# A buffer of its own for the last head's rows of wo, and kept keys in wo's fourth place

## The chip, the cores and the metric

The kernel runs on one core of a Trainium2 chip. The metric is the device time of one execution in microseconds, lower is better. Before the change three runs gave a median of 1353.76 us (1351.77 to 1354.28).

## The reference

One token goes through two equal rounds of attention over a cache of 8192 keys and values and an MLP, with the same weights in both rounds. All arrays are float32.

```python
B, Sq, D = 1, 1, 640
H, Sk, Dh = 32, 8192, 128            # Dff = 1728

def _A_ref(x, k_cache, v_cache, wq, wo):
    q = (x @ wq).reshape(B, Sq, H, Dh).transpose(0, 2, 1, 3)
    scores = jnp.einsum("bhqd,bhkd->bhqk", q, k_cache) * (Dh ** -0.5)
    p = _softmax(scores, axis=-1)
    o = jnp.einsum("bhqk,bhkd->bhqd", p, v_cache)
    return o.transpose(0, 2, 1, 3).reshape(B, Sq, H * Dh) @ wo

x = x + _A_ref(_layernorm(x), k_cache, v_cache, wq, wo)
x = x + relu(_layernorm(x) @ w1) @ w2
# and both lines once more
```

A head's keys and values are 8.39 MB, all heads' 268 MB, and each round needs all of them; what still lies on the chip from the first round needn't be read again in the second. A head's rows of wo are a block of 128 x 640, 327,680 bytes.

## The kernel before

**Loops.** `attention_and_mlp(L, ...)` is called for L = 0 and L = 1, called layers here. Layer 0 takes the heads from 0 to 31, layer 1 from 31 to 0. For each head the scores (line 433: `ps`, from keys and the spread query), a softmax, and the product with the values (line 484: `outs`) follow each other on TensorE, with VectorE and ScalarE in between.

**The ring.** Keys and values come in units (`UNITS`, line 41 on): a unit is one transfer and consists of pieces, each with its own products. A piece ("k", (r, c, n)) is n of 512 columns of quarter r. Most heads have two units of 4096 KB; heads 28 to 31 are cut finer. The units lie in one large buffer, `ring`, of RING = 4248 places (one place is 8 float32 in each of 128 partitions). `pump` (line 141) issues transfers on SP's queue in a fixed order as long as `place` (line 126) finds room; `release`, called when a piece's last product is recorded, frees its places and calls `pump`. In layer 0 the stream uses places 0 to 3072; the rest is for what stays.

**What stays.** `KEPT` and all units of heads 30 and 31 are read once, in layer 0, and used again in layer 1: `(29, 0)` are 176 columns of keys of head 29 (88 places), `(29, 5)` a quarter of a block of values (64 places). They lie from EDGE = 4096 on. In layer 1 `pieces_of` (line 195) takes a head's kept units first. The four units of head 29's keys that are not kept go, for layer 1, into buffers that the MLP of layer 0 no longer needs (`load_beside`, line 175: `mix`, `wct` and two parts of `w2_t`).

**wo.** The rows of wo come in groups of four heads, HG = 4, into one buffer `wo_t` (`load_wo`, line 211; 1280 KB, on ACT's queue but for the first). When a group's four heads are done, `run_out` (line 626) multiplies their outputs into `acc` (line 402) and then issues the load of the next group into the same buffer. That happens in the scores of the next group's first head: group 7 is loaded in head 28 of layer 0, and stays for the first four heads of layer 1. The layer's last head is multiplied on its own in `mlp` (line 766). Its rows are also needed early, for a product of wo and w1 (`mixing`, line 539); for that they are loaded a second time into `mix[:, :D]` (line 676), where VectorE then changes them in place.

**Side work.** `due` queues such jobs; `side_work` puts the next part of a job between two pieces of a head.

**Order and counters.** Each engine takes its instructions in the order of the program; so do the two queues, SP's and ACT's. Each transfer counts up one of eight counters (DMAHW0 to DMAHW7 in the listings) when it has landed. They are given out in turn over the transfers of both queues, in program order, so a transfer is not issued before the one eight places ahead has landed, whichever queue that was on.

Of the kernel before, what the change touches and what calls it, by code (L numbers as in the profile page):

```python
# [10 lines left out]
F32 = mybir.dt.float32  # L11
AF = mybir.ActivationFunctionType
ALU = mybir.AluOpType
AX = mybir.AxisListType

P = 128
D = 640
H = 32
# [5 lines left out]
HG = 4  # L24
NG = H // HG
# [8 lines left out]
RUN = COLS // 4  # L34
# [6 lines left out]
UNITS = {h: WHOLE for h in range(H)}  # L41
UNITS[0] = HALVES[:2] + LAST
UNITS[1] = HALVES
UNITS[29] = [
    ("k", [(0, 0, 176)]),
    ("k", [(0, 176, 336), (1, 0, 96)]),
    ("k", [(1, 96, 160)]),
    ("k", [(1, 256, 256), (2, 0, 384)]),
    ("k", [(2, 384, 128), (3, 0, RUN)]),
    ("v", [(0, 0, 1)]),  # L50
    ("v", [(0, 1, 3)]),
    ("v", V_ALL[1:2]),
# [2 lines left out]
UNITS[30] = HALVES  # L55
UNITS[28] = [("k", K_ALL[:1]), ("k", K_ALL[1:2])] + HALVES[1:]
UNITS[31] = HALVES[:2] + LAST
KEPT = [(29, 0), (29, 5)]
BESIDE = 4
RING = 4248  # L60
WC_AT = [5, 8]
MIX_AT = [[7, 9, 11, 13], [12, 16, 20, 24]]
FLAT = 3072
# [3 lines left out]
def wide(kind, piece):  # L67

    return 4 * piece[2] * (1 if kind == "k" else DH) // 8


def size(unit):
    return sum(wide(unit[0], piece) for piece in unit[1])
# [14 lines left out]
def decode_kernel(ctx: ExitStack, tc: tile.TileContext, x, kv, wq, wo, w1, w2, out):  # L88
    nc = tc.nc
    consts = ctx.enter_context(tc.tile_pool(name="consts", bufs=1))  # L90
# [10 lines left out]

    ring = consts.tile([P, 8 * RING], F32, name="ring")
    order = [(h, i) for h in range(H) for i in range(len(UNITS[h]))]
    kept = [u for u in order if u[0] > KEPT[0][0] or u in KEPT]
    assert sum(size(UNITS[h][i]) for h, i in kept) <= RING
    todo = [(0, u) for u in order]
    todo += [(1, (h, i)) for h in range(H)[::-1] for i in range(len(UNITS[h])) if (h, i) not in kept]

    beside = todo[len(order) : len(order) + BESIDE]
    del todo[len(order) : len(order) + BESIDE]  # L110
    dram_at, o = {}, 0
    for h, i in order:
        dram_at[h, i] = o
# [2 lines left out]
    at_of = {}  # L116
# [9 lines left out]
    def place(layer, u, n):  # L126


        step = 8 if u in KEPT else max(m for m in (8, 64, 256, 512) if n % m == 0)
        low, high = 0, RING if layer else FLAT  # L130
        if layer == 0 and u in kept and (u in KEPT or u[0] == 30 and UNITS[30][u[1]][0] == "k"):
            low, high = (EDGE, RING) if u in KEPT else (FLAT, EDGE)
        at, best = low, None
# [37 lines left out]
    def more_of_w2(a, b, where):  # L171
        rows = W2_LAST if a == FB - 1 else P
        nc.sync.dma_start(where[:rows], w2[:rows, a:b])

    def load_beside(i, where, n):
        (layer, u), at = beside[i], 0
        kind, pieces = UNITS[u[0]][u[1]]
        assert 8 * size(UNITS[u[0]][u[1]]) == n
        nc.sync.dma_start(
            where[:, at : at + n],  # L180
            kv[dram_at[u] : dram_at[u] + P * n].rearrange("(p m) -> p m", p=P),
        )
        for t, piece in enumerate(pieces):
            at_of[layer, u, t] = where, at
            at += 8 * wide(kind, piece)
# [18 lines left out]
    wq_t, wo_t = {}, {}  # L204
# [3 lines left out]
        wq_t[g] = t.rearrange("p (c n) -> p c n", c=NB)  # L208
        queue.dma_start(t, wq[P * g : P * g + P])

    def load_wo(g, queue):
        wo_t[g] = wts.tile([P, HG, D], F32, name="wo_t")
        queue.dma_start(wo_t[g], wo[g])

    xr = work.tile([P, DR], F32, name="xr", bufs=2)
    load_wq(0, nc.sync)
    nc.scalar.dma_start(xr, x)
    pump()
    load_wo(0, nc.sync)

    ones = consts.tile([P, 1], F32, name="ones")
    nc.vector.memset(ones, 1.0)
# [17 lines left out]
    w1_t = consts.tile([P, NB, DFF], F32, name="w1_t")  # L240
    w2_t = consts.tile([P, SLOTS, D], F32, name="w2_t")
    mix = consts.tile([P, DFF], F32, name="mix")
    wct = consts.tile([P, NB, P], F32, name="wct")


# [45 lines left out]
    def centred(xt, s):  # L291

        pt = columns(xt)
        mean(pt, s)
        yield "dve"
        return less_mean(pt, pt[:, :NB])
# [102 lines left out]
    def times_rows(acc, wt, col, first, last):  # L399

        for g in range(4):
            nc.tensor.matmul(  # L402
                acc[32 * g : 32 * g + 32, :DR],
                col.to_broadcast([col.shape[0], 32]),
                wt[:, g * DR : (g + 1) * DR],
                start=first,
                stop=last,
                skip_group_check=True,
            )
# [116 lines left out]

    o_cols = {}

    def projected(acc, run, cols, first, last):
        for j, h in enumerate(run):  # L530
            times_rows(
                acc,
                wo_t[h // HG][:, h % HG],
                cols[:, j : j + 1],
                first and j == 0,
                last and j == len(run) - 1,
            )

    def mixing():

        wc = mix[:, :D]
        s = work.tile([P, 1], F32, name="m_s")
        nc.vector.tensor_reduce(s, wc, AX.X, ALU.add)
        nc.vector.scalar_tensor_tensor(
            wc, s.to_broadcast([P, D]), -1.0 / D, wc, op0=ALU.mult, op1=ALU.add
        )
        yield "pe"
        pt = ps_m.tile([P, 512], F32, name="px")
        for c in range(4):
            nc.tensor.transpose(pt[:, c * P : (c + 1) * P], wc[:, c * DR : c * DR + P], ident)  # L550
        yield "dve"
        nc.scalar.copy(wct[:, :4].rearrange("p c d -> p (c d)"), pt)
        yield "pe"
        pt = ps_m.tile([P, 512], F32, name="px")
        for g in range(4):
            nc.tensor.matmul(
                pt[32 * g : 32 * g + 32, :P],
                wc[:, g * DR + P : (g + 1) * DR],
                ident,
                start=True,  # L560
                stop=True,
            )
        yield "dve"
        nc.scalar.copy(wct[:, 4], pt[:, :P])
# [28 lines left out]
    def attention_and_mlp(L, xr, s, before=None):  # L593

        heads = list(range(H))[:: 1 - 2 * L]
        last = heads[-1]
        runs = [heads[a : a + HG] for a in range(0, H, HG)]
        groups = [run[0] // HG for run in runs]
        runs[-1] = runs[-1][:-1]

        acc = ps_m.tile([P, 512], F32, name="acc")
# [18 lines left out]
        def queries_of(k):  # L620
            yield from wide_queries(groups[k], xc, r)
            yield "dve"
            if k + 1 < NG:
                load_wq(groups[k + 1], nc.scalar)

        def run_out(k):

            projected(acc, runs[k], o_cols[k], k == 0, False)
            yield "dve"
            load_wo(groups[k + 1], nc.scalar)  # L630

        def first_of_last():
            projected(acc, runs[-1][:2], o_cols[NG - 1], False, False)
            yield "dve"

        mlp_in = []

        def before_last():

            projected(acc, runs[-1][2:], o_cols[NG - 1][:, 2:], False, True)  # L640
            yield "dve"
            xp = work.tile([P, DR], F32, name="xr", bufs=2)
            sp = work.tile([P, 1], F32, name="x_s", bufs=2)
            nc.vector.scalar_tensor_tensor(
                xp, acc[:, :DR], 1.0, xr, op0=ALU.mult, op1=ALU.add, accum_out=sp
            )
            yield "pe"
            xpc = yield from centred(xp, sp)
            yield "pe"
            ph = ps_m.tile([P, 512], F32, name="acc")  # L650
            mlp_in.extend([xp, ph])
            for c in range(NB):
                hidden(ph, xpc[:, c : c + 1], w1_t[:, c], c == 0, False)
                if c < NB - 1:
                    yield "pe"

        def due(h):

            where = heads.index(h)
            k, j = divmod(where, HG)  # L660
            if j == 0:
                o_cols[k] = work.tile([P, HG], F32, name="o_cols", bufs=2)
            if where and j == 0:
                chores.append([run_out(k - 1), "pe"])
            if j == 2 and k + 1 < NG:
                slow.append([queries_of(k + 1), "pe"])
            if where == H - 2:
                chores.append([first_of_last(), "pe"])
            if where == H - 1:
                chores.append([before_last(), "pe"])  # L670
            if L == 0 and where == H - HG:
                slow.append([centre_query(NG - 1, HG - 1), "pe"])
            if L == 0 and where == 4:
                nc.scalar.dma_start(w1_t, w1)
            if where == WC_AT[L]:
                nc.scalar.dma_start(mix[:, :D], wo[last // HG][:, last % HG])
            if where == WC_AT[L] + 1:
                slow.append([mixing(), "dve"])
            if where in MIX_AT[L]:
                slow.append([mixing_quarter(MIX_AT[L].index(where)), "pe"])  # L680
# [28 lines left out]
        for where, h in enumerate(heads):  # L709
# [21 lines left out]
            if h == last:  # L731
                o = work.tile([P, 1], F32, name="c_ol")
# [16 lines left out]
            else:  # L749
                k, j = divmod(where, HG)  # L750
# [8 lines left out]
    def mlp(L, o, last, xp, ph):  # L759
# [3 lines left out]
        if L == 0:  # L763
            more_of_w2(SLOTS, 10, mix[:, : 2 * D].rearrange("p (b d) -> p b d", d=D))
        pd = ps_m.tile([P, 512], F32, name="pm")
        times_rows(pd, wo_t[last // HG][:, last % HG], o, True, True)
        in_wait(64)

        hr = wct.rearrange("p c d -> p (c d)")[:, : 2 * P]
# [99 lines left out]
        cols = work.tile([P, NB], F32, name="x_cols")  # L869
        nc.vector.tensor_copy(cols, pt[:, :NB])  # L870
        pq = ps_m.tile([P, 512], F32, name="px")
        for c in range(NB):
            g = c % 4
# [22 lines left out]
    s = work.tile([P, 1], F32, name="x_s", bufs=2)  # L896
# [84 lines left out]
```

## Time and profile before

| | |
|---|---|
| median of three runs | 1353.76 us |
| profiled execution | 1351.81 us, of it 1349.9 us span |
| TensorE busy | 909.9 us, 67% of the span |
| VectorE busy | 297.2 us, 22% |
| ScalarE busy | 58.5 us, 4% |
| moved by the transfers | 573.71 MB, mean 425 GB/s |
| mean granted clock of TensorE | 0.799 |

The page cuts the span into 40 equal slices of 33.7 us; its row "DMA" gives the busy share of the 16 DMA engines in tenths, its row "GB/s" what they moved. The chain of waits follows the work that ended last back to what released it; a share of "DMA" in it is time in which the next step waited for a transfer to land. q1 is SP's queue and q10 ACT's; their rows give packets, MB, and the share of the 16 engines' span.

### The profile page before, as it was taken

The page shows a single profiled execution, that of the slowest core. Times are in us where ns is not written, and L with a number is a line of the kernel's source. Part 1 is how long each engine was busy: PE and PEld are TensorE (multiplying, and loading weights), DVE is VectorE, ACT ScalarE, POOL GpSimd, SP SyncE. Part 2 cuts the span into 40 slices and gives each one's busy share as a digit, 9 for nine tenths or more (in the row PEclk, how much of TensorE's full clock was granted, in tenths as well). Part 3 has the DMA queues.
Part 4 walks back from the last instruction along what each step waited for, and adds up shares of the span by engine and source line. Part 5 has one row for each costly group of instructions (what it writes and reads, how often), then busy time and mean ns, then how long its engine had stood idle before and what let it go on. Part 6 is the DMA issues. An engine that isn't in the chain of part 4 may idle for free.

```text
span 1349.9 us, 14049 instructions
## 1 busy us (share of the span) xinstructions
PE 909.9 (67%) x6078; PEld 282.3 (21%) x6078; DVE 297.2 (22%) x979; ACT 58.5 (4%) x147; POOL 2.9 (0%) x10
## 2 busy tenths in 40 slices
PE   5564676766667666666688776677566767668667
PEld 2111121211112112112143211222112221122113
DVE  2121121222112222122223222221121212212212
ACT  0000000000000000000000000000000000000000
POOL 0000000000000000000000000000000000000000
PEclk8676788788777777777998876778778787787889
DMA  9999999999999999999999999999999999999997
GB/s 396 435 429 430 431 429 432 432 429 432 431 429 429 430 432 430 433 425 421 428 373 426 435 430 430 429 431 431 429 432 432 425 436 428 429 434 428 432 425 325
DMA packets 29605, 573.71 MB, mean 425 GB/s; under 512 B 3300, under 2 KB 3432, under 8 KB 6376
## 3 DMA queue, kind: packets, MB, share of 16 engines
q1 hardware_dynamic: 24936, 530.95, 91.9%
q10 hardware_dynamic: 4608, 41.86, 7.4%
q8 instruction: 48, 0.79, 0.2%
q14 instruction: 13, 0.11, 0.0%
HBM read 572.80 MB, written 0.00 MB: 424 GB/s over the span
## 4 chain that ended last, share of the span: by engine, by line
DMA 70%; PE 26%; DVE 2%; issue 1%; ACT 1%; SPq 0%; ACTq 0%; DVEq 0%
DMA ring<-in_kv 69%; PE outs L484 9%; PE ps L433 9%; PE px L571 2%; PE px L360 2%; DMA ring<-in_w 1%; PE acc L402 1%; PE pm L471 1%; PE px L374 1%; ACT p L459 0%; DVE h_t L445 0%; PE pm L450 0%; PE px L402 0%; DVE p L505 0%; DVE p L466 0%
## 5 line engine op out<-in xcount | busy, mean ns | idle before, releaser
L484 PE MATMUL outs<-ring,p 128*4 128x512 f32 (+2 forms) x2160 | 347.7, 773 | 162.4 <-DMA ring<-in_kv 109.7
L433 PE MATMUL ps<-ring,spread_q 128*32 128x512 f32 (+2 forms) x2056 | 334.0, 746 | 122.6 <-DMA ring<-in_kv 121.9
L445 DVE TENSOR_REDUCE h_t<-ps 128x1 f32<-128x512 f32 x64 | 44.3, 691 | 389.4 <-PE ps L433 389.3
L433 PEld LDWEIGHTS ps<-ring,spread_q 128*32 128x32 f32 x2056 | 71.6, 130 | 261.0 <-issue 229.1
L484 PEld LDWEIGHTS outs<-ring,p 128*4 128x4 f32 x2160 | 51.4, 96 | 325.5 <-issue 162.6
L459 ACT ACTIVATE p<-ps,h_t 128x512 f32<-128x512 f32 x63 | 43.3, 687 | 1179.0 <-DVE h_t L451 1179.0
L466 DVE STREAM_TRANSPOSE p<-p 128x128 f32<-128x128 f32 x256 | 79.8, 312 | 63.6 <-ACT p L459 56.9
L518 PE MATMUL pm<-ones,p 128*128 128x1 f32 (+1 forms) x128 | 24.7, 263 | 97.6 <-DVE p L505 97.6
L501 DVE TENSOR_SCALAR p<-outs,ind 128x128 f32<-128x128 f32 x64 | 22.5, 351 | 251.5 <-PE outs L484 251.5
L505 DVE SCALAR_TENSOR_TENSOR p<-outs,ind,p 128x128 f32<-128x128 f32 x188 | 66.0, 351 | 6.7
L450 PE MATMUL pm<-ident,h_t 128*128 128x128 f32 x128 | 31.2, 325 | 40.5 <-DVE h_t L445 40.4
L518 PEld LDWEIGHTS pm<-ones,p 128*128 128x128 f32 x128 | 19.2, 190 | 161.1 <-DVE p L505 160.3
L471 PEld LDWEIGHTS pm<-ind,h_t 128*128 128x128 f32 x128 | 27.4, 266 | 82.6 <-issue 82.6
L372 DVE TENSOR_SCALAR q_row<-px,ln_r 128x128 f32<-128x128 f32 x56 | 19.5, 349 | 109.1 <-PE ps L433 71.4
L571 PE MATMUL px<-w_t,wct 128*128 128x448 f32 (+1 forms) x80 | 43.4, 627 | 0.0
L360 PE MATMUL px<-wq_t,ln_xc 128*32 128x512 f32 x140 | 41.4, 921 | 0.0
L474 DVE RECIPROCAL h_t<-pm 128x1 f32<-128x1 f32 x64 | 10.7, 168 | 119.4 <-PE pm L471 119.4
L450 PEld LDWEIGHTS pm<-ident,h_t 128*128 128x128 f32 x128 | 19.0, 187 | 85.5 <-DVE h_t L445 83.8
L471 PE MATMUL pm<-ind,h_t 128*128 128x1 f32 x128 | 32.9, 326 | 0.0
L402 PE MATMUL acc<-wo_t,o_cols 128*32 128x160 f32 x496 | 31.1, 408 | 0.0
L402 PEld LDWEIGHTS acc<-wo_t,o_cols 128*32 128x32 f32 x496 | 24.3, 151 | 17.6 <-issue 14.2
L374 PEld LDWEIGHTS px<-sel,q_row 128*128 128x128 f32 x112 | 19.9, 221 | 35.1 <-DVE q_row L372 35.1
(126 smaller groups left out, 227.3 us busy)
## 6 DMA issues: line engine op xcount, KB each, us to landing
ring<-in_kv SPq DMA_DIRECT2D x104, 4096.0 KB, 28.8
ring<-in_kv SPq DMA_DIRECT2D x29, 2048.0 KB, 27.9
wq_t<-in_wq ACTq DMA_DIRECT2D x14, 1280.0 KB, 16.7
wo_t<-in_wo ACTq DMA_DIRECT2D x14, 1280.0 KB, 17.2
ring<-in_kv SPq DMA_DIRECT2D x9, 1024.0 KB, 14.9
w_t<-in_w SPq DMA_DIRECT2D x4, 1280.0 KB, 26.8
w_t<-in_w ACTq DMA_DIRECT2D x1, 4320.0 KB, 24.4
ring<-in_kv SPq DMA_DIRECT2D x5, 768.0 KB, 19.4
```

Of the source, the lines that this page charges most:

```text
L360: nc.tensor.matmul(pq[32 * strip : 32 * strip + 32], xc[:, c : c + 1].to_broadcast([P, 32]), wq_t[g][:, c], start=c < 4, stop=c in (1, 2, ...
L402: nc.tensor.matmul(acc[32 * g : 32 * g + 32, :DR], col.to_broadcast([col.shape[0], 32]), wt[:, g * DR : (g + 1) * DR], start=first, stop=last,
L433: nc.tensor.matmul(hd.ps[32 * g : 32 * g + 32, c : c + n], spread_q[:, 3 - r : 35 - r], tile_of[:, at + g * n : at + (g + 1) * n], start=f ...
L445: nc.vector.tensor_reduce(hd.nm, hd.ps, AX.X, ALU.max, negate=True)
L450: nc.tensor.matmul(pt[:, :P], hd.nm.to_broadcast([P, P]), ident, start=True, stop=True)
L459: nc.scalar.activation(hd.p, hd.ps, AF.Exp, bias=hd.low, scale=scale, accum_out=hd.l)
L466: nc.vector.transpose(hd.all_p[:, b * P : (b + 1) * P], hd.p[:, b * P : (b + 1) * P])
L471: nc.tensor.matmul(pt[:, :1], hd.l.to_broadcast([P, P]), ind[:, 4:5], start=True, stop=True)
L484: nc.tensor.matmul((hd.out if r0 < 2 else hd.out_2)[32 * g : 32 * g + 4, r0:r1].rearrange("p r d -> p (r d)"), hd.all_p[:, 32 * i : 32 * i ...
L505: nc.vector.scalar_tensor_tensor(oc, hd.out[:, r], ind[:, r : r + 1], oc, op0=ALU.mult, op1=ALU.add)
L518: nc.tensor.matmul(pt[:, :n], part, mask.to_broadcast([P, n]), start=i == 0, stop=i == len(parts) - 1,)
L571: nc.tensor.matmul(pt[:, :n], wct[:, c], w1_t[:, c, f : f + n], start=(c == 0), stop=(c == NB - 1),)
```

## The change

A new buffer `wo_last` holds the rows of wo of a layer's last head. They are loaded once in a layer, at the place where the load into `mix` stood, and serve the mixing and the product in `mlp`. So group 7 in layer 0 and group 0 in layer 1 are loaded without that head's rows. The fourth place of `wo_t`, free in group 7, takes 160 columns of head 29's keys, a unit that SP's stream no longer has (`BY_WO`); they stay there into layer 1. The ring is 80 places shorter, as much as `wo_last` takes. Of the 176 kept columns 16 remain in the ring; they are now the last 16 of quarter 3, a unit of their own.

```diff
 UNITS[29] = [
-    ("k", [(0, 0, 176)]),
-    ("k", [(0, 176, 336), (1, 0, 96)]),
-    ("k", [(1, 96, 160)]),
-    ("k", [(1, 256, 256), (2, 0, 384)]),
-    ("k", [(2, 384, 128), (3, 0, RUN)]),
+    ("k", [(0, 0, 160)]),
+    ("k", [(3, 496, 16)]),
+    ("k", [(0, 160, 352), (1, 0, 80)]),
+    ("k", [(1, 80, 160)]),
+    ("k", [(1, 240, 272), (2, 0, 368)]),
+    ("k", [(2, 368, 144), (3, 0, 496)]),
     ("v", [(0, 0, 1)]),
...
-KEPT = [(29, 0), (29, 5)]
+KEPT = [(29, 0), (29, 1), (29, 6)]
+BY_WO = KEPT[0]
...
-RING = 4248
+RING = 4168
...
-    todo = [(0, u) for u in order]
+    todo = [(0, u) for u in order if u != BY_WO]
...
+    def load_into(u, where, queue):
+        n = 8 * size(UNITS[u[0]][u[1]])
+        queue.dma_start(
+            where[:, :n], kv[dram_at[u] : dram_at[u] + P * n].rearrange("(p m) -> p m", p=P)
+        )
...
-    def load_wo(g, queue):
+    def load_wo(L, g, queue):
         wo_t[g] = wts.tile([P, HG, D], F32, name="wo_t")
-        queue.dma_start(wo_t[g], wo[g])
+        first, end = (L and g == 0), HG - (not L and g == NG - 1)
+        if end < HG:
+            load_into(BY_WO, wo_t[g][:, end], queue)
+            at_of[0, BY_WO, 0] = wo_t[g][:, end], 0
+        queue.dma_start(wo_t[g][:, first:end], wo[g][:, first:end])
+
+    def wo_of(L, h):
+        return wo_last if h == H - 1 or (L and h == 0) else wo_t[h // HG][:, h % HG]
...
+    wo_last = consts.tile([P, D], F32, name="wo_last")
...
-                wo_t[h // HG][:, h % HG],
+                wo_of(L, h),
...
-        nc.vector.tensor_reduce(s, wc, AX.X, ALU.add)
+        nc.vector.tensor_reduce(s, wo_last, AX.X, ALU.add)
         nc.vector.scalar_tensor_tensor(
-            wc, s.to_broadcast([P, D]), -1.0 / D, wc, op0=ALU.mult, op1=ALU.add
+            wc, s.to_broadcast([P, D]), -1.0 / D, wo_last, op0=ALU.mult, op1=ALU.add
         )
...
-                nc.scalar.dma_start(mix[:, :D], wo[last // HG][:, last % HG])
+                nc.scalar.dma_start(wo_last, wo[last // HG][:, last % HG])
...
-        times_rows(pd, wo_t[last // HG][:, last % HG], o, True, True)
+        times_rows(pd, wo_of(L, last), o, True, True)
```

Line numbers of the changed kernel lie 3 higher in `pump` and 15 higher in the products (line 433 is 448, 360 is 375, 374 is 389).

The ACT queue at the end of layer 0, before:

```order
L209 DMA wq_t<-in_wq 128x2560
L459 ACTIVATE p,h_t<-ps,h_t 128x512
L213 DMA wo_t<-in_wo 128x2560
L459 ACTIVATE p,h_t<-ps,h_t 128x512 x4
L213 DMA wo_t<-in_wo 128x2560
L459 ACTIVATE p,h_t<-ps,h_t 128x512 x4
```

and now:

```order
L215 DMA wq_t<-in_wq 128x2560
L474 ACTIVATE p,h_t<-ps,h_t 128x512
L224 DMA wo_t<-in_wo 128x2560
L474 ACTIVATE p,h_t<-ps,h_t 128x512 x4
L180 DMA wo_t<-in_kv 128x640
L224 DMA wo_t<-in_wo 128x1920
L474 ACTIVATE p,h_t<-ps,h_t 128x512 x4
```

The load of group 7 (the second one) has become two: the keys first, then three heads' rows.

SP's queue at head 29 of layer 0, with the counters that a transfer waits for in square brackets, before:

```order
L151 DMA ring<-in_kv 128x704
L151 DMA ring<-in_kv 128x1728 [waits DMAHW7_49,PE_49]
L151 DMA ring<-in_kv 128x640 [waits DMAHW0_49,PE_49]
L151 DMA ring<-in_kv 128x2560 [waits DMAHW1_49,PE_49]
L151 DMA ring<-in_kv 128x2560 [waits DMAHW2_49,PE_49]
L151 DMA ring<-in_kv 128x512 [waits DMAHW3_49]
L151 DMA ring<-in_kv 128x1536 [waits DMAHW4_49,PE_49]
```

and now:

```order
L154 DMA ring<-in_kv 128x64 [waits DMAHW7_49]
L154 DMA ring<-in_kv 128x1728 [waits DMAHW0_49,PE_49]
L154 DMA ring<-in_kv 128x640 [waits DMAHW1_49,PE_49]
L154 DMA ring<-in_kv 128x2560 [waits DMAHW2_49,PE_49]
L154 DMA ring<-in_kv 128x2560 [waits DMAHW3_49,PE_49]
L154 DMA ring<-in_kv 128x512 [waits DMAHW4_49]
L154 DMA ring<-in_kv 128x1536 [waits DMAHW5_49,PE_49]
```

The first row is the kept unit: 2816 bytes to a partition before, 256 now. With one transfer more, each counter has moved on by one. Counter 3 is, in both programs, that of the first load on ACT's queue in head 28: before the whole group of wo, which the 128x512 (the kept values) waited for; now the keys beside wo, which the last keys of head 29 (the second 128x2560) wait for. The three heads' rows behind them have counter 5, and the 128x1536 waits for that.

TensorE in head 29 of layer 1, before:

```order
L433 MATMUL ps<-ring,spread_q 32x176 x4
L360 MATMUL px<-wq_t,ln_xc 32x512 x5
L433 MATMUL ps<-mix,spread_q 32x336 x4
L374 MATMUL px<-sel,q_row 128x1
L433 MATMUL ps<-mix,spread_q 32x96 x4
L374 MATMUL px<-sel,q_row 128x1
```

and now:

```order
L448 MATMUL ps<-wo_t,spread_q 32x160 x4
L375 MATMUL px<-wq_t,ln_xc 32x512 x5
L448 MATMUL ps<-ring,spread_q 32x16 x4
L389 MATMUL px<-sel,q_row 128x1
L448 MATMUL ps<-mix,spread_q 32x352 x4
L389 MATMUL px<-sel,q_row 128x1
```

One piece more, of 16 columns, stands between the query's products (375) and the step that VectorE prepares from them (389); the steps behind have moved up by one piece.

More of the change, by code (lines that the diff above doesn't have):

```diff
@@ L104, in decode_kernel @@
     kept = [u for u in order if u[0] > KEPT[0][0] or u in KEPT]
-    assert sum(size(UNITS[h][i]) for h, i in kept) <= RING
-    todo = [(0, u) for u in order]
+    assert sum(size(UNITS[h][i]) for h, i in kept if (h, i) != BY_WO) <= RING
+    todo = [(0, u) for u in order if u != BY_WO]
+    n_first = len(todo)
     todo += [(1, (h, i)) for h in range(H)[::-1] for i in range(len(UNITS[h])) if (h, i) not in kept]
-    beside = todo[len(order) : len(order) + BESIDE]
-    del todo[len(order) : len(order) + BESIDE]
+    beside = todo[n_first : n_first + BESIDE]
+    del todo[n_first : n_first + BESIDE]
     dram_at, o = {}, 0
@@ L178, in load_beside @@
         assert 8 * size(UNITS[u[0]][u[1]]) == n
[L179 to L182, printed above, removed]
+        load_into(u, where, nc.sync)
         for t, piece in enumerate(pieces):
@@ L218, in decode_kernel @@
     pump()
-    load_wo(0, nc.sync)
+    load_wo(0, 0, nc.sync)
     ones = consts.tile([P, 1], F32, name="ones")
@@ L527, in decode_kernel, with projected @@
     o_cols = {}
-    def projected(acc, run, cols, first, last):
+    def projected(L, acc, run, cols, first, last):
         for j, h in enumerate(run):
@@ L626, in run_out @@
         def run_out(k):
-            projected(acc, runs[k], o_cols[k], k == 0, False)
+            projected(L, acc, runs[k], o_cols[k], k == 0, False)
             yield "dve"
-            load_wo(groups[k + 1], nc.scalar)
+            load_wo(L, groups[k + 1], nc.scalar)
         def first_of_last():
-            projected(acc, runs[-1][:2], o_cols[NG - 1], False, False)
+            projected(L, acc, runs[-1][:2], o_cols[NG - 1], False, False)
             yield "dve"
@@ L638, in before_last @@
         def before_last():
-            projected(acc, runs[-1][2:], o_cols[NG - 1][:, 2:], False, True)
+            projected(L, acc, runs[-1][2:], o_cols[NG - 1][:, 2:], False, True)
             yield "dve"
```

## The prediction

> **What bounds the kernel now.** I read the page first: the DMA row and the GB/s row of the slices, then the chain that ended last.
>
> ```profile
> span 1349.9 us, 14049 instructions
> DMA  9999999999999999999999999999999999999997
> GB/s 396 435 429 430 431 429 432 432 429 432 431 429 429 430 432 430 433 425 421 428 373 426 435 430 430 429 431 431 429 432 432 425 436 428 429 434 428 432 425 325
> DMA 70%; PE 26%; DVE 2%; issue 1%; ACT 1%; SPq 0%; ACTq 0%; DVEq 0%
> q1 hardware_dynamic: 24936, 530.95, 91.9%
> q10 hardware_dynamic: 4608, 41.86, 7.4%
> ```
>
> The transfers never pause except in three slices: the first, the one around the change of layer (373) and the last. Elsewhere they move some 430 GB/s, and the chain is 70% transfers. TensorE is busy for 67% of the span and waits for keys and values. So a byte less is worth its share of 430 GB/s wherever the chain stands on a transfer, and a delay of an engine costs only if it leaves the transfers nothing to do. The stretches that decide were asked for one by one (time of the stretch, busy time by engine, clock, DMA share, GB/s):
>
> ```profile
> 200.00:400.00 200.00, 131.98 (x826) 38.84 (x826) 40.80 (x130) 9.32 (x23) 0.00 (x0) 0.81 1.00 430
> ...
> 680.00:700.00 20.00, 17.19 (x242) 9.27 (x238) 5.86 (x24) 1.52 (x5) 0.00 (x0) 1.00 0.89 354
> ...
> 720.00:740.00 20.00, 17.19 (x148) 5.89 (x144) 5.92 (x19) 0.78 (x2) 0.00 (x0) 0.83 1.01 427
> ```
>
> Both ends of the two layers hang on transfers too. In the chain in order of time (start, length, what) the last one before the first layer's MLP, and the last two before the kernel's end, are:
>
> ```profile
> 649.60 37.51 DMA ring<-in_kv
> ...
> 1299.59 30.40 DMA ring<-in_kv
> ...
> 1330.05 15.50 DMA ring<-in_w
> ```
>
> **The bytes.** The change drops one head's rows of wo twice: head 31's from the last group of layer 0, head 0's from the last group of layer 1. One head's rows are 128 x 640 x 4 = 327,680 bytes; the one row loaded apart for the mixing was read before and still is, now into a buffer that stays. The keys kept between layers stay 176 columns (160 + 16), so k and v are read as often as before. That is 655,360 bytes less of 573.71 MB; at 430 GB/s 2 x 0.76 = **1.52 us less**. The layer 0 half comes ahead of the transfer that ends at 687.11, the layer 1 half ahead of the one that ends at 1345.55, so both should reach the end.
>
> **One transfer more.** The 16 columns come apart: 128 rows of 256 bytes. The two queue rows of the page price a packet: 16 engines x 1349.9 us x 91.9% = 24936 a + 530.95 MB x b, and with 7.4% the same for 4608 packets and 41.86 MB; solved, a is some 12 ns. 128 packets more over 16 engines are 8 x 12 ns = 0.1 us. Nothing in the trace isolates rows this short; ten times the price would be 1 us. I take **+0.1**.
>
> **The transfer that moves queue.** 160 columns of head 29's keys, which SP fetched well ahead into the ring, are now fetched on ACT's queue when head 28 has begun, into wo's fourth place. What stands around it in time:
>
> ```profile
> 620.10 0.34 ACTq L213 DMA_DIRECT2D wo_t<-in_wo  x1
> ...
> 637.77 4.17 PE L433 MATMUL ps<-ring,spread_q 128*32 128x176 f32 x48
> ...
> 643.02 1.28 PE L433 MATMUL ps<-ring,spread_q 128*32 128x128 f32 x16 [1.08 <-DMA ring<-in_kv]
> ```
>
> Issued at 620.1, it has 17.7 us until TensorE's first product of head 29 at 637.77, and that head's last keys aren't there before 643.02 anyway. How long such loads take (KB each, us to landing), the whole group first, then this very load, then the two loads of one head's rows:
>
> ```profile
> wo_t<-in_wo ACTq DMA_DIRECT2D x14, 1280.0 KB, 17.2
> ```
> ```profile
> wo_t<-in_wo ACTq DMA_DIRECT2D x1, 1280.0 KB, 11.7
> ```
> ```profile
> mix<-in_wo ACTq DMA_DIRECT2D x1, 320.0 KB, 15.9
> ```
> ```profile
> mix<-in_wo ACTq DMA_DIRECT2D x1, 320.0 KB, 23.3
> ```
>
> The 320 KB loads have the new transfer's shape, 2560 bytes to a partition, and take as long as 1280 KB in rows four times as long: beside SP's 32 KB rows a queue with short rows gets little. The 23.3 had a wo load ahead of it on its queue, issued 4.3 us before:
>
> ```profile
> 119.52 0.34 ACTq L213 DMA_DIRECT2D wo_t<-in_wo  x1
> ...
> 123.80 0.33 ACTq L676 DMA_DIRECT2D mix<-in_wo  x1
> ```
>
> The 15.9 had none. The new one has none ahead either, and SP's rows beside it are then at most 16 KB (2048 KB over 128 partitions), which is why the 1280 KB landed in 11.7 there. I expect 9 to 16 us, landing by 636: in time. That is a reason for the rival of the late keys, below.
>
> The Trainium skill, "DMA: Bandwidth & Descriptors", section "Queues, rings and completion order", speaks against the change here: each DMA engine turns round between its queues packet by packet, so a queue with short packets gets the smaller share beside one with long packets. The four rows above agree with it; the page gives no price for it, and the sum by it is that of the late keys if the landing slips past 19 us, and the forecast's if it doesn't.
>
> More is queued behind it than TensorE. SP's transfer of the last keys of head 29 shares a completion counter with it (the fence of SP's rows in the section on the change) and isn't issued before it has landed. Before, SP had the same wait one transfer later, for the whole wo load:
>
> ```profile
> SPq L151 <- DMA wo_t<-in_wo: 11.4, 1, 11.4
> ```
> ```profile
> ring<-in_kv SPq DMA_DIRECT2D x1, 1280.0 KB, 22.9
> ```
>
> There SP stood 11.4 us while 22.9 us of transfers were under way, and the rate hardly sagged:
>
> ```profile
> 620.00:624.00 4.00, 4.00 (x38) 1.83 (x34) 1.08 (x5) 0.00 (x0) 0.00 (x0) 1.00 0.99 421
> 624.00:628.00 4.00, 1.58 (x14) 0.41 (x10) 2.23 (x6) 0.78 (x2) 0.00 (x0) 0.92 1.00 418
> 628.00:632.00 4.00, 2.81 (x14) 0.61 (x10) 0.24 (x2) 0.00 (x0) 0.00 (x0) 0.65 1.02 419
> 632.00:636.00 4.00, 2.55 (x16) 0.36 (x16) 0.31 (x1) 0.00 (x0) 0.00 (x0) 0.78 1.01 417
> 636.00:640.00 4.00, 2.74 (x30) 1.80 (x34) 1.31 (x5) 0.00 (x0) 0.00 (x0) 0.50 1.02 419
> 640.00:644.00 4.00, 2.92 (x44) 1.07 (x32) 0.00 (x0) 0.00 (x0) 0.00 (x0) 0.87 1.02 419
> ```
>
> After the change less is under way during the wait. The 1280 KB transfer of 620.05 landed at 643.0; it is now the one that waits, and what is ahead of it ends 1.31 MB / 430 GB/s = 3.0 us sooner, less 0.8 us for the 320 KB that moved away: at 639.2. So if the new transfer lands by about 636 the queue never runs dry, and SP's next stop, for the other 960 KB of wo, finds the 1280 and 256 KB just issued (3.7 us) as cover. Cost **0**. From below, the sag itself bounds a gain: the six stretches lack 9, 12, 11, 13, 11 and 11 GB/s on 430, together 67 x 4 / 430 = 0.6 us. From above the next part has it. I take 0, since both wait patterns keep the same kind of load beside the stream.
>
> **Work on the engines.** TensorE gets four more products of 16 columns in each layer's head 29. In layer 1 those lie where TensorE, not a transfer, is the chain; the nearest rows:
>
> ```profile
> 736.91 0.37 PE L433 MATMUL ps<-mix,spread_q 128*32 128x96 f32 x8
> ...
> 737.73 0.48 PE L433 MATMUL ps<-wct,spread_q 128*32 128x160 f32 x8
> ```
>
> At most 0.4 us, and as much again where the query step behind the short piece has less to hide under. Cover: transfers issued just before are 18.9 us from landing, and the stretch 720 to 740 above runs at 427 GB/s. Without that cover it would be 0.8 us.
>
> ```profile
> ring<-in_kv SPq DMA_DIRECT2D x2, 2048.0 KB, 18.9
> ```
>
> The ring's 80 columns less cost nothing: they are the end in which the kept 88 lay, every other unit lies at the same place in both programs, and no transfer of more than the tail's 152 could have used it. VectorE's sum over one head's rows reads another buffer, with the same two instructions.
>
> **The sum.** -1.52 + 0.1 = -1.4 us: span 1349.9 to 1348.5, and with the 1.9 us around it 1351.81 to 1350.4. The profiled execution is 1.95 under the median of 1353.76, so the median becomes **1352.3**.
>
> **Rivals.** *The late keys (slower).* If the moved transfer takes the 23.3 us of the slower of its two likenesses, it lands at 643.4. Then SP's queue is empty from 639.2 on, 4.2 us; the 960 KB behind it on ACT's queue fill 2.3 us of that, and the restart costs up to 3.3 us (a 640 KB load alone, below, takes 4.8 us, of which 1.5 are data): +5.2, with the -1.4 1357.5. It decides from a landing later than 19 us after issue. For it: the likeness and the order of the queue. Against it: 11.7 us for four times the bytes at this very place.
>
> ```profile
> mix<-in_w SPq DMA_DIRECT2D x1, 640.0 KB, 4.8
> ```
>
> *The sag goes as well (faster).* SP gets past its 11.4 us stop sooner, the 0.6 us come back, and the cut wo loads leave more of the queue to long rows: -2.0, 1351.7, or with another half microsecond at the same wait in layer 1 1351.2. For it: 417 to 421 GB/s just there. Against: the sag lasts 12 us beyond the stop, so short rows rather than the stop may make it.
>
> *Half of it is lost.* The change of layer already leaves transfers idle (354 GB/s from 680 to 700); if that stretch simply grew by what layer 0 saves, 0.76 would remain: 1353.0. Against: the MLP starts from a transfer's landing, 649.60 + 37.51.
>
> **How the numbers follow.** Forecast 0.55, late keys 0.15, sag 0.22, half lost 0.08. No change within 0.2% means within 2.7 us here, about what a measurement can tell: the three runs shown lie 2.5 us apart. The forecast of -1.4 lies inside; with that scatter of the runs I give it a quarter of its weight beyond -2.7 and a twentieth beyond +2.7. The sag case I put beyond -2.7 six times in ten, the late keys beyond +2.7 three times in four, half lost almost never. Faster: 0.14 + 0.13 = 0.27; slower: 0.03 + 0.11 + 0.01 = 0.15; within: 0.58. The range goes from 1349.4 (the sag case with runs as low as the profiled one) to 1355.6 (late keys half paid); forecast alone, 1350.6 to 1354.
>
> **What would show it.** The page's bytes fall from 573.71 to 573.05 MB. The load of keys on ACT's queue lands before TensorE's first product of head 29, and TensorE doesn't wait for it. SP's wait for a wo load is shorter than 11.4 us or split in two. The stretches 620 to 644 stay at 417 GB/s or more; the change of layer stays as it is. I am wrong if a stretch there falls under 400, if the landing takes over 19 us, or if the bytes fall and the span doesn't.

## The result, and the profile after

Ten runs of the changed kernel gave a median of 1349.92 us (1349.51 to 1351.6), ten of the kernel before beside them 1353.65 us. The ratio is 0.9978, with a 95% interval of 0.9968 to 0.9987: faster, by 1.8 to 4.3 us. Forecast were 1352.3 us, 1.4 us less.

The page of the changed kernel, its span, slices, chain and queues:

```profile
span 1348.0 us, 14083 instructions
...
GB/s 396 436 431 431 429 428 427 430 433 429 432 429 432 428 433 431 429 430 416 428 380 424 434 430 429 430 431 431 430 432 430 425 435 431 429 430 432 432 422 328
DMA packets 29750, 573.06 MB, mean 425 GB/s; under 512 B 3444, under 2 KB 3576, under 8 KB 6776
...
q1 hardware_dynamic: 24936, 530.63, 92.0%
q10 hardware_dynamic: 4752, 41.54, 7.4%
...
DMA 70%; PE 26%; DVE 2%; issue 1%; ACT 1%; ACTq 0%; SPq 0%; DVEq 0%
```

The bytes fell from 573.71 to 573.06 MB, as counted; the rate did not move: 425 GB/s on the mean before and after, with the same three weak slices. The profiled spans differ by 1.9 us, more than the 1.5 us that the bytes are worth. Where does that stand? In the chain in order of time of the changed kernel, the landings that end layer 0 and the kernel:

```profile
522.10 26.74 DMA ring<-in_kv
...
649.09 37.00 DMA ring<-in_kv
...
1328.78 15.19 DMA ring<-in_w
```

The first one ends at 548.84 (522.10 + 26.74). The kernel before had 549.38 at that place (522.38 + 27.00), so 0.5 us of the difference arose before the first transfer that the change shortens, moves or adds. (Only one load of a head's rows into another buffer, at 123.80 in the kernel before, and the addresses behind the ring differ up to there.) In the three other profiles of the changed kernel this landing ends between 549.02 and 549.40, so half a microsecond comes and goes there with nothing changed. The last landing of layer 0 came at 686.09 against 687.11, 1.0 us earlier, and the last one of all at 1343.97 against 1345.55, 1.6 us. Less the 0.5 us, each layer gave some 0.5 us and 0.6 us. A single pair of traces can't tell that from 0.76 each. The traces of the experiments below say more on layer 0. TensorE's first product after the last landing of that layer starts between 686.75 and 687.24 in the four traces with all bytes. In the six with both rows dropped in which it waits for that landing, it starts between 686.20 and 686.43. On the mean that is 0.6 us earlier, and the two groups don't overlap.

The places that the prediction named are these. The keys beside wo on ACT's queue (KB, us to landing), then TensorE in head 29 of layer 0, from the timeline:

```profile
wo_t<-in_kv ACTq DMA_DIRECT2D x1, 320.0 KB, 7.8
```
```profile
622.33 0.33 ACTq L180 DMA_DIRECT2D wo_t<-in_kv  x1
...
637.19 0.48 PE L448 MATMUL ps<-wo_t,spread_q 128*32 128x160 f32 x8
637.49 2.65 PE L448 MATMUL ps<-ring,spread_q 128*32 128x16 f32 x48
641.97 1.28 PE L448 MATMUL ps<-ring,spread_q 128*32 128x144 f32 x16 [1.82 <-DMA ring<-in_kv]
```

They land at 630.2, 7 us before TensorE comes to them at 637.19; what it waits for in this head is, as before, the last piece, at 641.97. The moved transfer itself now stands in the chain of waits, ahead of the keys that share its counter:

```profile
622.33 7.85 DMA wo_t<-in_kv
630.24 11.68 DMA ring<-in_kv
```

By the chain alone one would say that this landing sets the pace here. The run with the keys on SP's queue, below, tests that. SP's waits for loads on ACT's queue, and the rate around them, first before, then now (stretch, its length, engines, clock, DMA share, GB/s):

```profile
SPq L154 <- DMA wo_t<-in_kv: 10.3, 1, 10.3
...
SPq L154 <- DMA wo_t<-in_wo: 2.2, 1, 2.2
```
```profile
620.00:644.00 24.00, 16.60 (x140) 6.08 (x136) 5.17 (x18) 0.78 (x2) 0.00 (x0) 0.79 1.01 419
```
```profile
620.00:644.00 24.00, 17.26 (x180) 7.16 (x172) 5.85 (x19) 0.78 (x2) 0.00 (x0) 0.86 1.01 418
```

The one stop of 11.4 us has become two, 10.3 and 2.2 us, and the rate there is 418 GB/s where the kernel before had 419 over the same 24 us (416 or 417 in the three other profiles of the change): the sag stayed. In head 29 of layer 1 the piece of 16 columns costs what was allowed for it:

```profile
734.93 0.21 PE L448 MATMUL ps<-ring,spread_q 128*32 128x16 f32 x2
735.54 0.38 PE L389 MATMUL px<-sel,q_row 128*128 128x1 f32 x2 [0.40 <-DVE q_row L387]
```

TensorE has nothing between the piece and the query step and waits 0.40 us for VectorE; the transfers run on (426 GB/s from 720 to 740).

### The profile page after: what moved, and what is told of

The parts are those of the page before. It is cut to its first block, busy times and chain, and to the rows that moved or that the text cites. A ratio compares the mean times of both kernels' runs of the same rounds, so it can differ in the third digit from the quotient of the medians.

```text
span 1348.0 us, 14083 instructions
## 1 busy us (share of the span) xinstructions
PE 922.5 (68%) x6094; PEld 288.0 (21%) x6094; DVE 297.1 (22%) x979; ACT 58.5 (4%) x147; POOL 2.9 (0%) x10
## 2 busy tenths in 40 slices
DMA packets 29750, 573.06 MB, mean 425 GB/s; under 512 B 3444, under 2 KB 3576, under 8 KB 6776
## 4 chain that ended last, share of the span: by engine, by line
DMA 70%; PE 26%; DVE 2%; issue 1%; ACT 1%; ACTq 0%; SPq 0%; DVEq 0%
DMA ring<-in_kv 67%; PE ps L448 10%; PE outs L499 8%; PE px L586 2%; PE px L375 2%; DMA ring<-in_w 1%; DMA wq_t<-in_wq 1%; PE acc L417 1%; PE pm L486 1%; DMA wo_t<-in_kv 1%; PE px L389 1%; DVE h_t L460 1%; ACT p L474 0%; PE pm L465 0%; DMA xr<-in_x 0%
## 5 line engine op out<-in xcount | busy, mean ns | idle before, releaser
L448 PE MATMUL ps<-ring,spread_q 128*32 128x512 f32 (+3 forms) x2056 | 339.4, 759 | 119.1 <-DMA ring<-in_kv 118.2
L417 PE MATMUL acc<-wo_t,o_cols 128*32 128x160 f32 x488 | 34.1, 443 | 0.0
L389 PEld LDWEIGHTS px<-sel,q_row 128*128 128x128 f32 x112 | 19.9, 222 | 34.5 <-DVE q_row L387 34.5
```

What stands on the lines that cost most here:

```text
L417: nc.tensor.matmul(acc[32 * g : 32 * g + 32, :DR], col.to_broadcast([col.shape[0], 32]), wt[:, g * DR : (g + 1) * DR], start=first, stop=last,
L448: nc.tensor.matmul(hd.ps[32 * g : 32 * g + 32, c : c + n], spread_q[:, 3 - r : 35 - r], tile_of[:, at + g * n : at + (g + 1) * n], start=f ...
```

## The experiments

Three theories stood against each other. A: only bytes count, and the rest of the first measurement is scatter. B: something else in the change gives another 0.6 to 1.6 us, such as the keys' move to another queue. C: the addresses of the buffers behind the shorter ring, which have shifted, do. Each run below is compared with the kernel before on the same chip.

**The change again.** The changed kernel as it stands, three more times.

> The changed kernel once more, as a control beside the next three. Forecast of the prediction (bytes only, -1.4 us, ratio 0.9990). First measurement: 0.9978 (0.9968 to 0.9987), and the two profiled spans differ by 1.9 us, of which 0.5 stood before the first instruction that the change touches. Theory A (bytes only, the rest is the scatter of the runs, which lie in two groups some 1.8 us apart for either kernel): between 0.9982 and 0.9992. Theory B (something beside the bytes gives 0.6 to 1.6 us: the keys' move to ACT's queue and SP's shorter stop) and theory C (the shorter ring shifts the buffers behind it, and the stream runs better from the start): again 0.9975 to 0.9983.

> The changed kernel a third time. The two measurements so far gave ratios of 0.9978 and 0.9987 to the kernel before. Theory A: 0.9983 to 0.9993, and within 0.5 us of the bytes alone beside it. Theories B and C: 0.9975 to 0.9983, and 0.6 to 1.6 us under the bytes alone.

> The changed kernel a fourth time, beside the three others. Ratios so far 0.9978, 0.9987, 0.9981. Theory A: 0.9984 to 0.9994. Theories B and C: 0.9977 to 0.9984.

The ratios were 0.9987 (0.9976 to 0.9997), 0.9981 (0.9973 to 0.9990) and 0.9984 (0.9975 to 0.9993). The first measurement, 0.9978, is the lowest of the four; their mean is 0.9983, or 2.4 us. The first repeat fell where A had asked, the second where B and C had, the third on the bound between them. That settles nothing by itself.

**The kernel before in the place of the one under test.**

> The kernel before, in the place of the kernel under test: what the comparison gives where nothing differs. No bias: ratio 0.9996 to 1.0004. If the remainder of 0.6 to 0.9 us beside the bytes comes from the comparison itself, it is seen here: 0.9993 to 0.9996.

0.9995 (0.9987 to 1.0004), though nothing differs: medians of 1352.59 and 1352.6, and 0.4 us between the means (1352.35 over 11 runs, 1352.79 over 33). So half a thousandth is within what the comparison gives for nothing; the interval holds 1 as well. Against this control the mean of the change measured beside it (1350.91) is 1.4 us lower; all 43 runs of the change have a mean of 1350.76, 1.6 us lower.

**The rows read again.** The change in everything but the bytes, run twice. In layer 0 the row comes back as one more load on ACT's queue:

```diff
-        first, end = (L and g == 0), HG - (not L and g == NG - 1)
+        first, end = 0, HG - (not L and g == NG - 1)
...
         queue.dma_start(wo_t[g][:, first:end], wo[g][:, first:end])
+        if end < HG:
+            queue.dma_start(wo_last, wo[g][:, end])
```

> The changed kernel, but the two heads' rows of wo are read a second time again (group 0 whole in layer 1; the last head's rows once more into their own buffer with group 7 in layer 0), 655,360 bytes back. Theory A: 1.5 us above the changed kernel, level with the kernel before (ratio to before 0.9995 to 1.0005). Theories B and C: the bytes return but the rest stays: 0.6 to 1.6 us under before (0.9988 to 0.9996).

> The changed kernel with both heads' rows read a second time, once more; first time 0.9996 (0.9987 to 1.0005) to the kernel before, by the mean over all runs 0.9 us under it. Theory A: 0.9995 to 1.0005, and 1.5 us above the change. Theories B and C: 0.9990 to 0.9995, 0.6 to 0.9 us under before.

0.9996 (0.9987 to 1.0005) and 0.9997 (0.9988 to 1.0005); the page shows 573.72 MB, the bytes of before. The mean over both, 22 runs, is 1352.48 us: 1.7 us above the change, and 0.1 us from the control's 1352.35. With the bytes back nothing of the gain over the control is left. The added load may have a small price of its own: in the first of the two traces the stretch from 620 to 644 ran at 410 GB/s, in the second at 416, in the change's four at 416 to 418. At 430 GB/s the 410 are worth 0.3 to 0.4 us.

**The bytes alone.** The kernel before with nothing but the two shortened loads, run twice. The last head of each layer is multiplied with a neighbour's rows, so its own part is left out of the output:

```diff
-        queue.dma_start(wo_t[g], wo[g])
+        first, end = (L and g == 0), HG - (not L and g == NG - 1)
+        queue.dma_start(wo_t[g][:, first:end], wo[g][:, first:end])
...
+        if h == H - 1 or (L and h == 0):
+            return wo_t[h // HG][:, 1]
```

> The kernel before, with nothing of the change but the two loads of wo cut to three heads' rows; the last head of each layer is multiplied with a neighbour's rows, so its own rows are left out of the output. Ring, kept keys and queues as before. Theory A: the whole of the change, -1.5 us (ratio 0.9985 to 0.9993), level with the change beside it. Theories B and C: -1.5 us, but 0.6 to 1.6 us slower than the change beside it.

> The two rows dropped from the kernel before and nothing else (of each layer's last head a neighbour's rows are used, its own are left out), once more, beside the third run of the change. It gave 0.9990. Theory A: 0.9985 to 0.9993, level with the change. Theories B and C: 0.6 to 1.6 us above the change.

0.9990 (0.9981 to 0.9999) and 0.9984 (0.9974 to 0.9993), mean 1351.29 us over 22 runs. The change's 1350.76 is 0.5 us lower, with a standard error of 0.4 us (how far chance alone moves such a difference of means): no difference that the runs can tell, though one of half a microsecond isn't excluded. The second pair, 0.6 us apart by their means, just reaches what B and C had asked for; the first, 0.2 us apart, doesn't.

**More bytes.** From the bytes alone, every load of wo on ACT's queue one row shorter; a quarter of wo is left out of the output:

```diff
-        first, end = (L and g == 0), HG - (not L and g == NG - 1)
+        first, end = (1, HG) if L and g == 0 else (0, HG - 1 if g or L else HG)
...
-        if h == H - 1 or (L and h == 0):
+        if h % HG == HG - 1 or (L and h == 0):
```

> The kernel before, with each of the fourteen loads of wo on ACT's queue cut to three heads' rows; every fourth head is multiplied with a neighbour's rows, so a quarter of wo is left out of the output. 14 x 327,680 bytes less than before. Theory A (a byte costs its share of 430 GB/s wherever it is dropped): 10.7 us less (ratio 0.9921, within 0.0010). If a dropped row is worth more than its bytes (short rows on ACT's queue holding up the stream): 15 us or more less, below 0.989. If part of the bytes is hidden anyway: 8 us or less.

0.9925 (0.9912 to 0.9937) from five runs, or 10.1 us less (8.5 to 11.9), where 14 rows at 430 GB/s are 10.7. The page shows 569.13 MB. On the mean a row dropped is worth 0.72 us (0.61 to 0.85), and its bytes, 0.76, lie in that.

**The addresses.** `wo_last` right behind the ring, so that w1, w2 and `mix` lie where they lay before:

```diff
     ring = consts.tile([P, 8 * RING], F32, name="ring")
+    wo_last = consts.tile([P, D], F32, name="wo_last")
...
-    wo_last = consts.tile([P, D], F32, name="wo_last")
```

> The changed kernel with the buffer for the last head's rows placed right behind the shortened ring, so that the MLP's weights and the mixing buffer lie at the addresses of the kernel before. So far the change is 2.6 us under before over 32 runs, the bytes alone 2.0 us over 22. Theory A (bytes only): level with the change beside it, within 0.6 us. Theory C (addresses): 0.6 to 0.9 us above the change.

0.9985 (0.9977 to 0.9994), beside the change's 0.9984. By the means the two are 0.1 us apart (1350.99 and 1350.91), so the addresses have nothing to explain that the runs can tell.

**The keys on SP's queue.**

```diff
-            load_into(BY_WO, wo_t[g][:, end], queue)
+            load_into(BY_WO, wo_t[g][:, end], nc.sync)
```

> The changed kernel, but the 160 columns beside wo are fetched on SP's queue, at the same place in the program. They then stand behind some 20 us of transfers, land some 5 to 8 us after TensorE comes to head 29, and TensorE waits for them. Theory A and C: level with the changed kernel within 0.3 us, since the stream goes on. Theory B: 0.6 to 1.6 us slower than the changed kernel. The rival of the late keys (a late landing empties SP's queue): 2 to 5 us slower.

0.9984 (0.9975 to 0.9993), level with the change. The waits of TensorE and the rate after:

```profile
PE ps L448 <- DMA wo_t<-in_kv: 7.4, 1, 7.4
```
```profile
620.00:644.00 24.00, 13.22 (x108) 5.27 (x100) 5.18 (x18) 0.78 (x2) 0.00 (x0) 0.78 1.01 417
644.00:680.00 36.00, 28.81 (x250) 11.24 (x250) 8.79 (x30) 1.56 (x4) 0.00 (x0) 0.87 1.01 429
```

Here the keys are late: TensorE stands 7.4 us for them. The stream runs on at 417 and 429 GB/s, TensorE catches up in the idle time it has anyway, and the time doesn't change (1351.21 us on the mean, the change beside it 1351.24). So the queue that carries the keys makes no difference that the runs can tell, and the landing that stood in the chain doesn't set the time. SP's stop for a wo load is a single one of 11.8 us here, and that makes no difference either. Theory B is left without the cause that it named.

**The keys much later.** Still on SP's queue, but issued when head 29 begins:

```diff
-            load_into(BY_WO, wo_t[g][:, end], queue)
...
             due(h)
+            if not L and h == BY_WO[0]:
+                load_into(BY_WO, wo_t[NG - 1][:, HG - 1], nc.sync)
             hd = Head(h)
```

> The changed kernel, but the 160 columns beside wo are fetched on SP's queue just before head 29, behind all that SP has issued ahead by then: some 25 us after TensorE comes to head 29. What SP issues next needs places that head 29 must free first. If only an empty queue costs: the transfers run dry when the keys land and start again when TensorE has freed the first places, 4 to 9 us above the changed kernel, far less than TensorE's wait of 20 to 30 us. If TensorE's wait itself costs: 15 us or more. If late keys cost nothing at all: within 0.5 us.

1375.48 us from five runs, ratio 1.0164 (1.0150 to 1.0178): 25 us above the change, where I had expected 4 to 9. The profile is that of the longest of the five, 1380.36 us, with a span 30.6 us above the change's, so its sum has to reach 30.6 and not 25. The waits, and the rate in the stretches around them; behind them the same stretches of the change:

```profile
PE ps L447 <- DMA wo_t<-in_kv: 34.5, 1, 34.5
```
```profile
SPq L154 <- PE ps L447: 46.1, 7, 32.8
```
```profile
640.00:664.00 24.00, 0.00 (x0) 0.00 (x0) 0.00 (x0) 0.00 (x0) 0.00 (x0) 0.50 1.02 432
...
664.00:676.00 12.00, 4.35 (x56) 2.68 (x60) 0.00 (x0) 0.00 (x0) 0.00 (x0) 0.50 0.33 138
676.00:680.00 4.00, 3.19 (x26) 1.21 (x16) 0.98 (x2) 0.07 (x1) 0.00 (x0) 0.81 0.61 188
680.00:704.00 24.00, 18.83 (x143) 6.16 (x146) 7.08 (x24) 1.48 (x4) 0.00 (x0) 0.93 0.99 406
704.00:724.00 20.00, 17.73 (x238) 9.30 (x230) 5.18 (x20) 1.52 (x5) 0.00 (x0) 1.00 0.16 57
724.00:760.00 36.00, 30.51 (x302) 12.86 (x302) 10.07 (x42) 1.65 (x4) 1.10 (x2) 0.86 0.99 380
```
```profile
664.00:676.00 12.00, 7.54 (x46) 2.54 (x46) 3.76 (x13) 0.78 (x2) 0.00 (x0) 1.00 1.01 429
...
680.00:704.00 24.00, 21.76 (x292) 11.25 (x292) 5.63 (x23) 1.52 (x5) 0.55 (x1) 1.00 0.93 359
704.00:724.00 20.00, 16.40 (x188) 6.94 (x180) 7.11 (x28) 0.87 (x2) 0.55 (x1) 1.00 1.01 423
724.00:760.00 36.00, 27.35 (x208) 9.02 (x208) 9.92 (x33) 2.33 (x6) 0.00 (x0) 0.81 1.02 432
```

From 640 to 664 TensorE does nothing at all and the stream runs at 432 GB/s: the wait by itself costs no transfer. The first gap was foreseen: SP stands 32.8 us for places that TensorE must free, and from 664 to 676 the stretch lacks (430 - 138) x 12 / 430 = 8.1 us, with 2.3 us more in the four us behind. The second was not: from 704 to 724 another 17.3 us are missing, and 4.2 in the 36 us behind. At the end of layer 0 the ring fills with keys and values that stay, nothing is left to fetch, and the MLP of layer 0 begins only when TensorE is through. What TensorE is still late by then shows as an empty queue. The change lacks 4.0 us from 680 to 704 and 0.2 in the rest; this kernel lacks 1.3 from 680 to 704. 8.1 + 2.3 + 1.3 + 17.3 + 4.2 less the change's 4.2 are 29.0 of the 30.6 us; the other 1.6 us are not accounted for. By its number alone the run would come near the theory that TensorE's wait of 34.5 us itself costs; the full rate under that wait and the missing transfers behind it speak for the empty queue. I had looked for them in one place only.

## Why the prediction was right

**The bytes (-1.52 us): right, and shown.** Both rows reach the end. Putting them back costs 1.7 us and leaves the kernel level with the control; dropping them alone gives the gain, within half a microsecond; 14 rows give 14 times one row's price within the interval. The rival "half of it is lost" falls with that: it left 0.76 us for the two rows, or 0.38 a row.

**One transfer more (+0.1): not told apart.** The page counts 144 more packets on q10, where 128 had been expected, 144 more under 512 bytes and the same number on q1. At the estimated 12 ns that is still 0.1 us over 16 engines. The change isn't slower than the bytes alone, so the extra transfer and the extra piece together cost less than the runs can resolve; ten times the price, the 1 us of the upper bound, is not what they show.

**The moved transfer (0): right in its effect, mostly too long in its time.** I expected a landing 9 to 16 us after issue, from the two loads of the same shape. It took 7.8, and 7.9 to 9.7 in the profiles of the six other runs with the keys there on ACT's queue; four of the seven lie under 9. The 320 KB loads elsewhere ran beside SP's rows of 32 KB, this one beside rows of 16 KB and less. I had named that difference and still stayed too near the slow rows, but no run tries the row length alone. The seven loads were issued between 619.8 and 622.5 and landed between 629.4 and 630.6: the later issues took the shorter times. So the landing is set in part by something outside the load, and that stays open.

**The two rivals about it.** The sag stayed (418 against 419 GB/s) and the rows put back gave the control's time, so the faster rival had no cause. The slower one needed a landing 19 us after issue; it came at 8 to 10. What a late landing costs was tried in another form than the rival had it, with TensorE late rather than SP's queue stopped by a counter: 7.4 us cost nothing, 34.5 us cost 25 by the median. The price of 5.2 us for a queue emptied by the counter wasn't tried.

**Work on the engines (0): right.** 0.21 us at the piece's end and 0.40 us of waiting in layer 1, with the stream at 426 GB/s. (The prediction's "80 columns" by which the ring is shorter are 80 places; nothing hangs on it.)

**The sum and the size.** The forecast was 1352.3 and the first median 1349.92, 3.7 us under the kernel before and so past the 2.7 that I had called no change. It lies inside the range, but under the 1350.6 where the range of the forecast alone began; that lower end had been kept for the sag case, which didn't come about. That the first median fell inside is in part luck. The medians of the three repeats were 1350.52, 1350.34 and 1351.16.

How large the gain is depends on what stands beside it. Read against the control it is 1.6 us, from 43 and 11 runs, with a standard error of 0.3 us, and the forecast of 1.4 lies in it. Against all 97 runs of the kernel before that stood beside these measurements (mean 1353.10) it is 2.4 us. But the rows put back are 0.6 us under those 97 as well, and the control, in which nothing differs, 0.8 us. So what goes beyond the bytes shows up without the change too, and nothing of the change that was tried explains it; chance or the place in the comparison would do, and the runs don't tell these apart. The step from the rows put back to the change needs neither reference: 1.7 us, with a standard error of 0.3, where the bytes were put at 1.5.

One part of the scatter can be seen. The prediction has both ends of the layers hang on transfers. In the profile above the kernel's last products start on a landing; in the first repeat of the same kernel, with a span of 1349.3 us, they start behind TensorE's own work, 1.3 us later:

```profile
1328.78 15.19 DMA ring<-in_w
...
1344.01 0.93 PE px L417 x16
```
```profile
1344.09 1.22 PE px L417 x32
...
1345.33 0.93 PE px L417 x16
```

Of the change's four profiles two end on the landing (spans 1348.0 and 1348.4) and two on TensorE (both 1349.3). The end is nearly a tie, and a byte less helps there only when the landing is the later of the two.

## What to carry to other kernels

Where the transfers never pause, count the bytes first: two dropped rows and fourteen were worth their share of 430 GB/s within the intervals, and moving a transfer to another queue or TensorE 7 us late made no difference that the runs could tell. Lateness gets its price where the stream has a pause to fall into, as at the change of layer here, so look for the next such pause before calling a wait free. For gains of a thousandth, run the old kernel against itself in the same comparison; here it gave half a thousandth for no difference at all, about as much as had seemed to want a cause beside the bytes. And when a sum of gaps is set against a time, take the time of the profiled execution: here it was 5 us above the median.

## What the runs showed of the hardware

The time from issue to landing of the same 320 KB in rows of 2560 bytes on ACT's queue went from 7.8 us beside rows of at most 16 KB on SP's queue (up to 9.7 in other runs) to 15.9 us beside rows of 32 KB, and to 23.3 us with 1280 KB ahead on its own queue. While they were under way the transfers moved 413 GB/s (622 to 631 us), 423 (831 to 847) and 429 (124 to 147). With TensorE idle for 24 us the stream still ran at 432 GB/s; it fell to 57 where nothing was left to fetch.
